# Tap-diagonal matmuls merged into larger runs, two transposes moved together and three filler matmuls added at the start of a convolution-plus-MLP kernel

## The chip, the cores and the metric

The kernel runs on one core of one Trainium2 chip. The metric is the device time of one execution in microseconds (us), as the median of several executions. A trace of one execution has its own clock, the *span*, from the first instruction to the last; it is about 1.8 us shorter than the device time (687.26 against 685.5 us in the profiled run of before). All positions below are us from the start of the span.

The engines are called by the profile's names: PE is the tensor engine, PEld its weight loads, ACT the scalar engine, DVE the vector engine, POOL GpSimd.

## The reference

```python
# x: (8, 4096, 192), weight: (8 heads, 7 taps)
w = exp(weight - max); w = w / (sum(w) + 1e-9)          # softmax over the 7 taps
out = einsum('hk,bskhg->bshg', w, windows_of(x))        # causal 7-tap convolution, a filter per head
# 32768 tokens of 192, d_ff = 2048
h = out @ w_in                                          # 192 -> 2048
g = h * sigmoid(beta * h)                               # beta per column of h
return g @ w_out                                        # 2048 -> 192
```

## The kernel before

The 32768 tokens are handled as two streams of 16384. Most of the time goes to 512-token steps: the DVE forms the seven-tap sum of x (tile `xc`), the PE multiplies by `w_in` into PSUM (`ph`), the ACT applies Silu (`g`), and the PE multiplies by `w_out` (`po`). The first steps are smaller: 128, 128 and 256 tokens, then four of 256. For the first three the PE does the convolution too, as matmuls with diagonal matrices of taps, because that is available sooner. That start is what the change touches.

```python
def warm(n, cols):                      # filler matmuls, result never read
    for _ in range(n):
        pin(nc.tensor.matmul(idle[:, 0, 0:cols], ones[:, 0:128], ones[:, 0:cols], start=True, stop=True))

warm(9, 256)
...
def conv_0(cv, b, k0=0, k1=K):          # two matmuls a tap, one for each stream
    for k in range(k0, k1):
        for s in range(NS):
            pin(nc.tensor.matmul(cv[s][:, 0:NK * 128], diag[half_of(s), k, :, :]...,
                xr[half_of(s), :, 128 * b + k:128 * b + k + 128], start=(k == 0), stop=(k == K - 1)))
...
t = transpose_0(pa[0], x0, 0)           # block 0: three transposes on the PE
take_0(t, 0, act=True)
warm(7, 128)
...
conv_0(b0, 0)                           # the first convolution, seven taps, nothing between them
...
def mm1_pair(i, u):                     # "large pair": two columns of w_in, one PSUM tile
    ph = psum_h.tile([128, NS, TILE], FP32, name="ph")       # psum_h has two buffers
    ...  6 matmuls, then 2 activations of 256 columns
...
for u in range(NF // 2):                # steps 0, 1 and 2
    mm1_pair(i, u)
    first_tile(i, u)                    # pieces of the convolution of blocks 1, 2, 3 (the change)
    ...  mm2 of earlier steps, as first_mm2 says
```

`first_tile(i, u)` is the list that the change rewrites. "Pair (0,5)" below means `mm1_pair(0, 5)`.

Of the kernel before, what the change touches and what calls it, by code (L numbers as in the profile page):

```python
# [19 lines left out]
def kernel(  # L20
# [9 lines left out]
    nc = tc.nc  # L30

    B, S, D = x.shape
    H, K = weight.shape
# [3 lines left out]
    NF = F // 128  # L37
    NK = 3
    Q = D // NK
    NS = 2  # L40
# [5 lines left out]
    def pin(ins):  # L46

        return tc.keep_in_program_order(ins)
# [27 lines left out]
    def load_x(j, s, b0=0, b1=NB, eng=None):  # L76
        if j not in xf_of:
            xf_of[j] = xf_pool.tile([128, NB, NS, D], FP32, name="xf")
        src = xs[s, TILE * j + 128 * b0:TILE * j + 128 * b1, :]
        pin((eng or nc.sync).dma_start(out=xf_of[j][:, b0:b1, s, :],  # L80
                                       in_=src.rearrange("(b p) d -> p b d", p=128)))

    def cast_x(j, s, b0=0, b1=NB, eng=None):
        if j not in xbf_of:
            xbf_of[j] = xbf_pool.tile([128, NB, NK, NS, Q], BF16, name="xb")
        pin((eng or nc.vector).tensor_copy(  # L86
            xbf_of[j][:, b0:b1, :, s, :].rearrange("p b k q -> p k b q"),
            xf_of[j][:, b0:b1, s, :].rearrange("p b (q k) -> p k b q", k=NK)))

    def new_xt(j):  # L90
        xt_of[j] = xt_pool.tile([128, NK, LEAD + TILE], BF16, name="xt")

    def transpose_x(j, b):
        if j not in xt_of:
            new_xt(j)
        c = LEAD + 128 * b
        pin(nc.sync.dma_start_transpose(
            out=xt_of[j][:, :, c:c + 128],
            in_=xbf_of[j][:, b, :, :, :].rearrange("p k s q -> p (k s q)")))
# [9 lines left out]
    def half_of(s):  # L109
        return slice(64 * s, 64 * s + 64)  # L110
# [9 lines left out]
    xb0 = consts.tile([128, 2, NS, D], BF16, name="xb0")  # L120
# [52 lines left out]
    def po_banks():  # L173
        return [po_bank(), po_bank()]
# [7 lines left out]
    def warm(n, cols):  # L182
        for _ in range(n):
            pin(nc.tensor.matmul(idle[:, 0, 0:cols], ones[:, 0:128], ones[:, 0:cols], start=True, stop=True))
# [3 lines left out]
    nmax = consts.tile([128, 1], FP32, name="nmax")  # L188
    tap_ps = cv0[:, 1, 0:K]
    pin(nc.tensor.matmul(tap_ps, sel.rearrange("h s g j -> h (s g j)"), taps, start=True, stop=True))  # L190
    pin(nc.vector.tensor_reduce(out=nmax, in_=tap_ps, axis=AX.X, op=ALU.max, negate=True))
    etap = consts.tile([128, K], FP32, name="etap")
    tsum = consts.tile([128, 1], FP32, name="tsum")
# [14 lines left out]
    def transpose_0(bank, src, b):  # L208

        bf = src.dtype == BF16  # L210
        t = (bank.bitcast(BF16) if bf else bank)[:, 0:NK * 128].rearrange("p (k t) -> p k t", k=NK)
        v = src[:, b, :, :].rearrange("p s d -> p (s d)").rearrange("p (m k) -> p k m", k=NK)
        for kk in range(NK):
            pin(nc.tensor.transpose(t[:, kk, :], v[:, kk, :], ident_b if bf else ident))
        return t

    def take_0(t, b, act=False):
        dst = xr[:, :, PAD + 128 * b:PAD + 128 * b + 128]
        if act:
            pin(nc.scalar.activation(dst, t, AF.Copy))  # L220
        else:
            pin(nc.vector.tensor_copy(dst, t))

    def conv_0(cv, b, k0=0, k1=K):

        for k in range(k0, k1):
            for s in range(NS):
                pin(nc.tensor.matmul(  # L228
                    cv[s][:, 0:NK * 128], diag[half_of(s), k, :, :].rearrange("p s q -> p (s q)"),
                    xr[half_of(s), :, 128 * b + k:128 * b + k + 128], start=(k == 0), stop=(k == K - 1)))  # L230

    def evac_0(cv, b, s, eng, k0=0, k1=NK):
        i, c = place[b]
        src = cv[s][:, 128 * k0:128 * k1].rearrange("p (k t) -> p k t", t=128)
        dst = xc_of[i][:, s, k0:k1, c:c + 128]
        if eng is nc.scalar:
            pin(nc.scalar.activation(dst, src, AF.Copy, scale=rsum))
        else:
            pin(eng.tensor_scalar_mul(dst, src, rsum))

    new_xt(0)
    pa = po_banks()
    pb = po_banks()
# [27 lines left out]
    def scale_w_out(c):  # L271
        pin(nc.vector.tensor_scalar_mul(w_out_s[:, c, :], w_out_f[:, c, :], rbeta[:, c:c + 1]))
# [219 lines left out]

    def first_tile(i, u):
        if (i, u) == (0, 1):
            conv_0(pb, 1, 0, 2)
        elif (i, u) == (0, 2):
            conv_0(pb, 1, 2, 4)
        elif (i, u) == (0, 3):
            take_0(transpose_0(pa[0], xb0, 0), 2)
            conv_0(pb, 1, 4, 5)  # L500
        elif (i, u) == (0, 4):
            take_0(transpose_0(pa[1], xb0, 1), 3)
            conv_0(pb, 1, 5, K)
            for s in range(NS):
                evac_0(pb, 1, s, nc.vector)
            for c in range(4):
                scale_w_out(c)
        elif (i, u) == (0, 5):
            conv_0(pa, 2, 0, 2)
        elif (i, u) == (0, 6):  # L510
            conv_0(pa, 2, 2, 5)
        elif (i, u) == (0, 7):
            conv_0(pa, 2, 5, K)
            for s in range(NS):
                evac_0(pa, 2, s, nc.vector)
            for c in range(4, 8):
                scale_w_out(c)
        elif (i, u) == (1, 0):
            conv_0(pb, 3, 0, 2)
        elif (i, u) == (1, 1):  # L520
            conv_0(pb, 3, 2, 5)
        elif (i, u) == (1, 2):
            conv_0(pb, 3, 5, K)
            for s in range(NS):
                evac_0(pb, 3, s, nc.vector)
            for c in range(8, NF):
                scale_w_out(c)
        elif (i, u) == (1, 6):
            new_xt(1)
            ts_ = [transpose_0(pb[b], xb1, b) for b in range(2)]  # L530
            for b in range(2):
                pin(nc.vector.tensor_copy(xt_of[1][:, :, LEAD + 128 * b:LEAD + 128 * b + 128], ts_[b]))
            pin(nc.vector.tensor_copy(xt_of[0][:, :, TILE + LEAD - PAD:],
                                      xr[:, :, TILE:].bitcast(FP32)))
        elif (i, u) == (1, 7):
            for s in range(NS):
                cast_x(1, s, 2, NB)
            for b in range(2, NB):
                transpose_x(1, b)
            for j in (2, 3):  # L540
                for s in range(NS):
                    load_x(j, s)
# [2 lines left out]

    prs_0 = ((0, 0), (1, 0))
    first_mm2 = {}
    for key, us, cuts in (((0, 0), [(1, u) for u in range(3, 8)], (0, 4, 8, 12, 13, 16)),
                          ((1, 0), [(2, 1), (2, 2)], (0, 8, 16)),
                          ((0, 1), [(2, 3), (2, 4)], (0, 8, 16)),  # L550
                          ((1, 1), [(2, 5), (2, 6), (2, 7)], (0, 5, 10, 16))):
        for (i, u), c0, c1 in zip(us, cuts, cuts[1:]):
            first_mm2[(i, u) + key] = range(c0, c1)

    for i in range(n_steps):
        plan = mm2_plan(i - 1) if NP <= i <= NQ else [[] for _ in range(NF)]
        new_g(i, 0)
        if i < NP:
            new_g(i, 1)
        if i < NP:  # L560
            for u in range(NF // 2):
                mm1_pair(i, u)
                first_tile(i, u)
                for ph in (0, 1):
                    for j in range(i):
                        for fc in first_mm2.get((i, u, j, ph), ()):
                            mm2(j, prs_0, ph, fc)
                if i == 2:
                    vector_work(i, 1300, flush=u == NF // 2 - 1)
            continue  # L570
        for u in range(NF):
            if u == NF // 2:
                new_g(i, 1)
            mm1(i, u)
            for t in plan[u]:
                mm2(i - 1, *t)
                if t[1] == 1 and t[2] == NF - 1:
                    budget -= 2 * (D + 60) / 0.96
            if i > NQ:
                mm2_quarters(NM)  # L580
            vector_work(i, 1307 * steps[i][1] // TILE, flush=u == NF - 1)
# [30 lines left out]
```

## Time and profile before

| what | value |
|---|---|
| device time, three runs | 687.62 to 687.64 us, median 687.63 |
| span of the profiled run | 685.5 us |
| first activation of step 0 | 8.63 us |
| tap sum of the second 512-token step complete | 90.59 us (88.52 + 2.07 below) |
| first activation of that step | 91.16 us |
| from there to the end | 594.3 us |

The busy time of each engine in four stretches of the kernel before (columns: stretch, its length, then busy us and instruction count of PE, PEld, DVE, ACT and POOL, then the granted tensor clock, DMA share and GB/s):

```profile
8.63:12.63 4.00, 3.87 (x48) 2.47 (x44) 1.40 (x6) 3.86 (x10) 3.57 (x5) 1.00 1.14 254
12.63:21.57 8.94, 8.94 (x138) 7.04 (x135) 8.32 (x27) 8.35 (x22) 3.19 (x5) 1.00 1.05 256
21.57:90.64 69.07, 68.47 (x1270) 59.41 (x1266) 68.29 (x118) 68.23 (x97) 0.00 (x0) 1.00 0.47 128
90.64:670.00 579.36, 579.36 (x10728) 410.65 (x10731) 466.31 (x730) 497.81 (x448) 0.00 (x0) 1.00 0.36 90
```

In the third stretch PE, DVE and ACT all look full. A share cannot tell which of them sets the pace; the waits can. In the fourth the PE alone is full. The timeline of the ACT before (start, duration, what, count, and in brackets the idle time before it with its releaser):

```profile
8.63 4.00 ACT L323 ACTIVATE gp<-ph,beta 128x256 bf16<-128x256 f32 x10 [0.54 <-PE ph L319]
12.97 8.81 ACT L323 ACTIVATE gp<-ph,beta 128x256 bf16<-128x256 f32 x22 [0.35 <-PE ph L319]
74.16 16.36 ACT L340 ACTIVATE g<-ph,beta 128x1024 bf16<-128x1024 f32 x16 [0.35 <-PE ph L336]
91.16 2.34 ACT L340 ACTIVATE g<-ph,beta 128x1024 bf16<-128x1024 f32 x2 [0.64 <-PE ph L336]
```

At 91.16 the ACT waited for the PE, and the PE timeline of before shows why: it waited for the DVE's tap sum.

```profile
89.63 0.76 PE L336 MATMUL ph<-xc,w_in_s 64*64 64x512 bf16 x8
90.64 0.41 PE L336 MATMUL ph<-xc,w_in_s 64*64 64x512 bf16 x4 [0.25 <-DVE xc L302]
```

The DVE timeline of before, from its last start-up work (the eviction of block 3 at 17.20 us, that is, its copy out of PSUM) to that tap sum:

```profile
17.20 1.14 DVE L239 TENSOR_SCALAR xcp<-po,rsum 128x384 bf16<-128x384 f32 x2 [0.25 <-PE po L228]
18.25 1.96 DVE L272 TENSOR_SCALAR w_out_s<-w_out_f,rbeta 128x192 bf16<-128x192 f32 x8
20.25 0.62 DVE L532 COPY xt<-po 128x384 bf16<-128x384 bf16 x2
21.57 0.50 DVE L86 CAST xb<-xf 128x384 bf16<-128x384 f32 x1 [0.21 <-DMA xf<-in_x_dram]
22.18 0.75 DVE L300 TENSOR_SCALAR acc<-xt,tapn 128x768 f32<-128x768 bf16 x1
...
88.52 2.07 DVE L302 SCALAR_TENSOR_TENSOR xc<-xt,tapn,acc 128x512 bf16<-128x512 bf16 x3
```

Last, two lines of the PE timeline in the first convolution of before. Successive taps start 0.32 us apart; later in the trace a tap takes 0.18 us. The tensor clock is at half rate here.

```profile
5.38 0.52 PE L228 MATMUL po<-xr,diag 64*128 64x384 f32 x1
5.70 0.52 PE L228 MATMUL po<-xr,diag 64*128 64x384 f32 x1
```

### The profile page before, as it was taken

How to read it: one execution, taken by the hardware profiler on the slowest of the kernel's cores; microseconds unless marked ns; L12 is line 12 of the kernel's file. 1: busy time of each engine (PE TensorE's matmuls, PEld its weight loads, DVE VectorE, ACT ScalarE, POOL GpSimd, SP SyncE). 2: the span in 40 equal slices, each digit the busy share in tenths (PEclk: the TensorE clock that was granted, in tenths of full speed). 3: DMA queues.
4: the chain of work that ended last, by engine and by line, in shares of the span. 5: the costliest groups of instructions: out<-in, count | busy, mean ns of one | idle time of the engine just before them, and what ended most of it. 6: DMA issues, size and time to landing. Idle time of an engine off the chain costs nothing.

```text
span 685.5 us, 26898 instructions
## 1 busy us (share of the span) xinstructions
PE 681.0 (99%) x12365; PEld 497.0 (73%) x12365; DVE 552.8 (81%) x906; ACT 583.9 (85%) x585; POOL 14.5 (2%) x26
## 2 busy tenths in 40 slices
PE   9999999999999999999999999999999999999998
PEld 7799767777777777777777777777777777777777
DVE  5999999999988889878889888889888888875102
ACT  7999988888888888888888888888888888888881
POOL 8000000000000000000000000000000000000000
PEclk9999999999999999999999999999999999999999
DMA  9664334354423344423344323444323443220213
GB/s 201 176 164 121 96 93 104 86 118 117 114 75 71 100 112 117 104 64 87 102 116 118 93 68 91 103 117 118 81 65 102 106 117 72 59 54 9 49 48 93
DMA packets 149872, 66.82 MB, mean 97 GB/s; under 512 B 112592, under 2 KB 149152, under 8 KB 149760
## 3 DMA queue, kind: packets, MB, share of 16 engines
q1 hardware_dynamic: 146448, 61.08, 35.5%
q0 software_dynamic: 3168, 3.93, 2.8%
q8 instruction: 96, 1.57, 1.0%
q14 instruction: 16, 0.13, 0.1%
q10 hardware_dynamic: 144, 0.10, 0.1%
HBM read 28.32 MB, written 25.17 MB: 78 GB/s over the span
## 4 chain that ended last, share of the span: by engine, by line
PE 86%; DVE 9%; DMA 2%; issue 1%; POOL 1%; POOLq 0%; DVEq 0%
PE po L414 42%; PE ph L336 42%; DVE acc L302 5%; PE po L452 2%; DMA xf<-in_x_dram 1%; DMA w_in_s<-in_moe_w_in_dram 1%; DVE o_sp L374 1%; DVE xb L86 1%; DVE acc L300 1%; DVE xc L302 1%; POOL w_in_s L113 0%; DVE w_out_q L275 0%; POOL xb L131 0%; POOL sel L146 0%; DVE xt L291 0%
## 5 line engine op out<-in xcount | busy, mean ns | idle before, releaser
L340 ACT ACTIVATE g<-ph,beta 128x1024 bf16<-128x1024 f32 (+1 forms) x528 | 557.4, 1062 | 82.3 <-PE ph L336 65.2
L336 PE MATMUL ph<-xc,w_in_s 64*64 64x512 bf16 (+2 forms) x5856 | 624.6, 369 | 0.6 <-ACT g L323 0.3
L414 PE MATMUL po<-g,w_out_q 64*64 64x512 bf16 x5376 | 578.9, 376 | 0.0
L336 PEld LDWEIGHTS <-w_in_s 64*64 64x64 bf16 (+1 forms) x5856 | 320.8, 104 | 105.5 <-issue 1.4
L414 PEld LDWEIGHTS <-w_out_q 64*64 64x64 bf16 x5376 | 312.4, 105 | 67.5
L302 DVE SCALAR_TENSOR_TENSOR acc<-xt,tapn,acc 128x512 f32<-128x512 bf16 (+1 forms) x455 | 311.1, 752 | 0.6
L431 DVE STREAM_TRANSPOSE o_sb<-po 128x512 f32<-128x512 f32 x84 | 74.4, 886 | 113.0 <-PE po L414 112.9
L302 DVE SCALAR_TENSOR_TENSOR xc<-xt,tapn,acc 128x512 bf16<-128x512 bf16 (+1 forms) x91 | 64.0, 754 | 0.1
L86 DVE CAST xb<-xf 128x768 bf16<-128x768 f32 (+1 forms) x62 | 48.3, 816 | 0.2 <-DMA xf<-in_x_dram 0.2
L300 DVE TENSOR_SCALAR acc<-xt,tapn 128x512 f32<-128x512 bf16 (+1 forms) x91 | 40.5, 480 | 1.1
L368 PE MATMUL po<-w_out_s,g 64*128 64x192 bf16 x640 | 41.2, 243 | 0.0
L368 PEld LDWEIGHTS <-g 64*128 64x128 bf16 x640 | 31.3, 94 | 3.5
L374 DVE COPY o_sp<-po 128x192 f32<-128x192 f32 x32 | 10.2, 350 | 7.3 <-PE po L452 7.3
L319 PE MATMUL ph<-xcp,w_in_s 64*128 64x256 bf16 (+1 forms) x144 | 14.7, 306 | 0.2
L323 ACT ACTIVATE gp<-ph,beta 128x256 bf16<-128x256 f32 x32 | 12.4, 479 | 1.3 <-PE ph L319 0.9
L452 PEld LDWEIGHTS <-g 128*128 128x128 bf16 x128 | 10.5, 98 | 0.4 <-issue 0.4
L452 PE MATMUL po<-w_out_s,g 128*128 128x192 bf16 x128 | 10.7, 246 | 0.0
L323 ACT ACTIVATE g<-ph,beta 128x512 bf16<-128x512 f32 x16 | 9.6, 691 | 0.1
L319 PEld LDWEIGHTS <-w_in_s 64*128 64x128 bf16 x144 | 6.7, 94 | 3.3 <-issue 0.9
L228 PE MATMUL po<-xr,diag 64*128 64x384 f32 x49 | 8.8, 398 | 0.0
L368 PE MATMUL po<-w_out_s,gp 64*128 64x192 bf16 x128 | 7.7, 243 | 0.0
L368 PEld LDWEIGHTS <-gp 64*128 64x128 bf16 x128 | 6.0, 94 | 1.8
(53 smaller groups left out, 61.5 us busy)
## 6 DMA issues: line engine op xcount, KB each, us to landing
xf<-in_x_dram SPq DMA_DIRECT2D x60, 384.0 KB, 4.6
out_dram<-o_sb SPq DMA_DIRECT2D x112, 192.0 KB, 4.3
out_dram<-o_sp SPq DMA_DIRECT2D x12, 192.0 KB, 4.3
xt<-xb SPq DMA_TRANSPOSE x122, 2.4
w_out_f<-in_moe_w_out_dram POOLq DMA_DIRECT2D x4, 384.0 KB, 7.0
w_in_s<-w_in_s POOLq DMA_DIRECT2D x4, 192.0 KB, 7.1
out_dram<-o_sp SPq DMA_DIRECT2D x8, 96.0 KB, 1.6
w_in_s<-in_moe_w_in_dram POOLq DMA_DIRECT2D x4, 144.0 KB, 5.2
```

Of the source, the lines that this page charges most:

```text
L86: pin((eng or nc.vector).tensor_copy(xbf_of[j][:, b0:b1, :, s, :].rearrange("p b k q -> p k b q"), xf_of[j][:, b0:b1, s, :].rearrange("p b ...
L300: pin(nc.vector.tensor_scalar_mul(a, src, w))
L302: pin(nc.vector.scalar_tensor_tensor(out=xc_of[i][:, k0:k1, 0:n] if k == K - 1 else a, in0=src, scalar=w, in1=a, op0=ALU.mult, op1=ALU.add))
L319: pin(nc.tensor.matmul(ph[:, h, 0:NS * n], w_in_s[half_of(h), kk, ts(fcs[h], 128)], xc_of[i][half_of(h), :, kk, :], start=(kk == 0), stop= ...
L323: pin(nc.scalar.activation(g_at(i, fcs[h])[:, :, 0:n], ph[:, h, 0:NS * n].rearrange("p (s t) -> p s t", s=NS), AF.Silu, scale=beta[:, fcs[ ...
L336: pin(nc.tensor.matmul(ph[m0:m1, s, 0:n], w_in_s[half_of(s), kk, 128 * fc + m0:128 * fc + m1], xc_of[i][half_of(s), kk, 0:n], start=(kk == ...
L340: pin(nc.scalar.activation(g_at(i, fc)[:, :, 0:n], ph[:, :, 0:n], AF.Silu, scale=beta[:, fc:fc + 1]))
L368: pin(nc.tensor.matmul(po[q][:, 0:D], g_at(i, fc)[r, s, ts(b, 128)], w_out_s[r, fc, :], start=(phase == 0 and fc == 0), stop=(phase == 1 a ...
L374: pin(nc.vector.tensor_copy(dst, po[:, 0:D]))
L414: pin(nc.tensor.matmul(po_of[i, m][half_of(s), 0:n], w_out_q[half_of(r), fc, m, :], g_at(i, fc)[half_of(r), s, 0:n], start=(first and fc = ...
L431: pin(nc.vector.transpose(osb_of[i][:, 0:n // L, :, m], po_of[i, m][:, 0:n].rearrange("p (b l) -> p b l", l=L)))
L452: pin(nc.tensor.matmul(po[:, 0:D], g_at(i, fc)[:, s, ts(b, 128)], w_out_s[:, fc, :], start=(fc == 0), stop=(fc == NF - 1)))
```

## The change

The intent: fewer changes between the small diagonal matmuls and the large pairs (ten runs become six), block 1 finished before the PE turns to the late transposes, and three fillers so that the PE has no thin spot before the first transposes. The last part, a new distribution of the first `mm2` over the pairs of step 1, follows from block 3's being finished two pairs earlier.

```diff
--- before.py
+++ after.py
@@ -188,6 +188,7 @@
     nmax = consts.tile([128, 1], FP32, name="nmax")
     tap_ps = cv0[:, 1, 0:K]
     pin(nc.tensor.matmul(tap_ps, sel.rearrange("h s g j -> h (s g j)"), taps, start=True, stop=True))
+    warm(3, 128)
     pin(nc.vector.tensor_reduce(out=nmax, in_=tap_ps, axis=AX.X, op=ALU.max, negate=True))
     etap = consts.tile([128, K], FP32, name="etap")
     tsum = consts.tile([128, 1], FP32, name="tsum")
@@ -492,38 +493,30 @@
 
     def first_tile(i, u):
         if (i, u) == (0, 1):
-            conv_0(pb, 1, 0, 2)
+            conv_0(pb, 1, 0, 4)
         elif (i, u) == (0, 2):
-            conv_0(pb, 1, 2, 4)
+            conv_0(pb, 1, 4, K)
         elif (i, u) == (0, 3):
-            take_0(transpose_0(pa[0], xb0, 0), 2)
-            conv_0(pb, 1, 4, 5)
-        elif (i, u) == (0, 4):
-            take_0(transpose_0(pa[1], xb0, 1), 3)
-            conv_0(pb, 1, 5, K)
+            t23 = [transpose_0(pa[b], xb0, b) for b in range(2)]
+            for b in range(2):
+                take_0(t23[b], 2 + b)
             for s in range(NS):
                 evac_0(pb, 1, s, nc.vector)
+        elif (i, u) == (0, 5):
+            conv_0(pa, 2, 0, 4)
+        elif (i, u) == (0, 6):
+            conv_0(pa, 2, 4, K)
+            for s in range(NS):
+                evac_0(pa, 2, s, nc.vector)
             for c in range(4):
                 scale_w_out(c)
-        elif (i, u) == (0, 5):
-            conv_0(pa, 2, 0, 2)
-        elif (i, u) == (0, 6):
-            conv_0(pa, 2, 2, 5)
         elif (i, u) == (0, 7):
-            conv_0(pa, 2, 5, K)
-            for s in range(NS):
-                evac_0(pa, 2, s, nc.vector)
-            for c in range(4, 8):
-                scale_w_out(c)
+            conv_0(pb, 3, 0, 4)
         elif (i, u) == (1, 0):
-            conv_0(pb, 3, 0, 2)
-        elif (i, u) == (1, 1):
-            conv_0(pb, 3, 2, 5)
-        elif (i, u) == (1, 2):
-            conv_0(pb, 3, 5, K)
+            conv_0(pb, 3, 4, K)
             for s in range(NS):
                 evac_0(pb, 3, s, nc.vector)
-            for c in range(8, NF):
+            for c in range(4, NF):
                 scale_w_out(c)
         elif (i, u) == (1, 6):
             new_xt(1)
@@ -545,7 +538,7 @@
 
     prs_0 = ((0, 0), (1, 0))
     first_mm2 = {}
-    for key, us, cuts in (((0, 0), [(1, u) for u in range(3, 8)], (0, 4, 8, 12, 13, 16)),
+    for key, us, cuts in (((0, 0), [(1, u) for u in range(2, 8)], (0, 3, 6, 9, 12, 13, 16)),
                           ((1, 0), [(2, 1), (2, 2)], (0, 8, 16)),
                           ((0, 1), [(2, 3), (2, 4)], (0, 8, 16)),
                           ((1, 1), [(2, 5), (2, 6), (2, 7)], (0, 5, 10, 16))):
```

## The prediction

> **What bounds the kernel.** I read three stretches off the timeline and the table of busy time by stretch.
> - 8.63 to about 90 us: the ScalarE activations run nearly back to back (0.40 us each in the first two steps, 0.65 us in the 256-row steps). Their only recorded waits for TensorE are 0.54 us at 8.63, 0.35 at 12.97, 0.35 at 74.16 and 0.64 at 91.16.
> - 21.57 to 90.6 us: VectorE is busy 68.29 of 69.07 us. It starts when a DMA delivers `xf`: issued at 12.68, landed 8.86 us later, and VectorE had waited 0.21 us for it. It ends with `xc` at 90.6 us, for which TensorE waits 0.25 us. The chain of waits runs through exactly these pieces.
> - 90.64 to 670 us: TensorE is busy all the time (579.36 of 579.36 us).
>
> **What the change does.** It touches only the first 21 us. No work is removed; three matmuls of 128 columns are added.
> - *Fewer switches on TensorE.* Diagonal runs of 2 taps (4 matmuls) take 0.44 us to the next pair's start and runs of 3 taps (6) take 0.62, so a pair of matmuls costs 0.09 x 2 and each run carries about 0.08 us of its own (estimate from these two). Ten runs become six: about 0.3 us less. The two late transposes each begin 0.43 us after their pair where a diagonal run begins 0.25 after: one such 0.18 us goes. Together about 0.5 us of TensorE time between 8 and 17 us.
> - *Block 1 finished before the transposes*, block 3 two pairs earlier. ScalarE's 0.35 us wait at 12.97 should go. The seven-tap halves (8 matmuls, about 0.80 us) plus a pair (0.25) exceed ScalarE's 0.80 us per pair, but two buffers absorb it; perhaps 0.1 to 0.2 us returns as a wait near pair (1,0).
> - *Fillers.* At 2.8 to 3.3 us TensorE has little work. The diagonal pairs at 4.90 to 6.98 come every 0.32 us, later ones every 0.18: half clock, then full. The Trainium skill, "TensorE: Matmul & The Clock Gate", Part 1, says a busy window of about 3.4 us is needed to leave half rate and that the window runs freely; this trace agrees with the two rates, but not necessarily with a moved switch. If the fillers fill the deciding window, up to 1.1 us goes from the first convolution; otherwise they cost up to 0.3 us. I lean slightly to no effect.
> - *VectorE.* Its twelve remaining output-weight scalings (0.245 us each) now stand in one run after block 3's eviction. I estimate that eviction at about 16.1 us and VectorE ready for `xf` at about 21.1, still before 21.55.
>
> **How much is critical.** TensorE and ScalarE get ahead by 0.3 to 1 us by 17 us, but step 90.6 us waits for VectorE's sum of taps, whose start is set by a DMA that no TensorE instruction releases and whose 69 us are saturated. So the gain turns into a longer wait of TensorE for `xc` near 90 us. The total hardly moves.
>
> **Prediction.** 687.5 us, 80% range 687.0 to 687.8. Faster by over 2%: 0.005; within 2%: 0.99; slower by over 2%: 0.005.
>
> **What would show each step.** The first activation of step 0 at 8.63 us or earlier; the 0.35 us wait at 12.97 gone; VectorE's second `xf` cast still starting at 21.5 to 21.6 after a DMA wait; the tap sum ending at 90.5 to 90.7; TensorE's wait for `xc` there grown from 0.25 us; the stretch after it unchanged at about 595 us.
>
> **What would make it wrong.** `xf` landing at another time; block 3's eviction after 16.5 us, so that VectorE reaches `xf` late (slower by that much); a VectorE chain with hidden waits for TensorE (faster, at most about 1 us); the clock falling back to half rate.

## The result

The change is neutral. In the same rounds the changed kernel took 687.76 us (687.23 to 688.16, 4 runs) and the kernel before 687.62 (687.52 to 687.64, 4 runs). The ratio is 1.0002, with a 95% interval from 0.9984 to 1.0019. (A ratio here is the mean time of one kernel's fast runs over the mean of the other's fast runs of the same rounds, so it is not quite the ratio of the two medians.) What stands out is the spread: 0.9 us for the changed kernel. It is not the change's own: in the three later sets of rounds the nine runs of the kernel before spread over 0.8 to 1.4 us.

The lines of the changed kernel that answer to those above; its source lines are numbered one higher from the fillers on. First the ACT timeline:

```profile
8.81 4.82 ACT L324 ACTIVATE gp<-ph,beta 128x256 bf16<-128x256 f32 x12 [0.54 <-PE ph L320]
13.96 1.72 ACT L324 ACTIVATE gp<-ph,beta 128x256 bf16<-128x256 f32 x4 [0.33 <-PE ph L320]
15.91 6.30 ACT L324 ACTIVATE gp<-ph,beta 128x256 bf16<-128x256 f32 x16 [0.23 <-PE ph L320]
74.49 16.36 ACT L341 ACTIVATE g<-ph,beta 128x1024 bf16<-128x1024 f32 x16 [0.35 <-PE ph L337]
91.27 2.34 ACT L341 ACTIVATE g<-ph,beta 128x1024 bf16<-128x1024 f32 x2 [0.42 <-PE ph L337]
```

The start is 0.18 us later. The wait at 12.97 is gone, but two others came, 0.33 us before pair (0,6) and 0.23 before pair (1,0). At 74 us the ACT is 0.33 us behind before; at 91 us only 0.11, because the wait there fell from 0.64 to 0.42 us. The DVE and PE timelines of the changed kernel:

```profile
16.31 1.14 DVE L240 TENSOR_SCALAR xcp<-po,rsum 128x384 bf16<-128x384 f32 x2
20.69 0.62 DVE L525 COPY xt<-po 128x384 bf16<-128x384 bf16 x2 [0.49 <-PE po L215]
21.30 0.89 DVE L86 CAST xb<-xf 128x384 bf16<-128x384 f32 x2
22.31 0.75 DVE L301 TENSOR_SCALAR acc<-xt,tapn 128x768 f32<-128x768 bf16 x1
...
88.64 2.07 DVE L303 SCALAR_TENSOR_TENSOR xc<-xt,tapn,acc 128x512 bf16<-128x512 bf16 x3
```

```profile
3.31 0.50 PE L184 MATMUL ph<-const-bfloat16-1.0 128*128 128x128 bf16 x3
3.61 0.85 PE L215 MATMUL po<-ident,x 128*128 128x128 f32 x3
5.62 0.52 PE L229 MATMUL po<-xr,diag 64*128 64x384 f32 x1
5.94 0.52 PE L229 MATMUL po<-xr,diag 64*128 64x384 f32 x1
...
90.76 0.41 PE L337 MATMUL ph<-xc,w_in_s 64*64 64x512 bf16 x4 [0.17 <-DVE xc L303]
```

Three things are visible. Block 3's eviction (the 16.31 line) did come earlier than before (17.20 us). The DVE's chain of tap sums nevertheless began 0.13 us later (22.31 against 22.18). And the fillers delayed the first transposes by 0.30 us, from 3.31 to 3.61, while the taps still come 0.32 us apart, so they did not bring the full clock earlier in this execution. The stretch from the first activation near 91 us to the end is 594.3 us in both traces.

### The profile page after: what moved, and what is told of

It reads as the page before. It is cut to its first block, busy times and chain, and to the rows that moved or that the text cites. A ratio compares the mean times of both kernels' runs of the same rounds, so it can differ in the third digit from the quotient of the medians.

```text
span 685.6 us, 26903 instructions
## 1 busy us (share of the span) xinstructions
PE 681.1 (99%) x12368; PEld 498.1 (73%) x12368; DVE 552.4 (81%) x906; ACT 583.8 (85%) x585; POOL 14.5 (2%) x26
## 4 chain that ended last, share of the span: by engine, by line
PE 89%; DVE 9%; issue 1%; ACT 0%; DVEq 0%
PE po L415 42%; PE ph L337 42%; DVE acc L303 5%; PE po L453 2%; DVE xb L86 1%; DVE o_sp L375 1%; PE ph L320 1%; DVE acc L301 1%; DVE xc L303 1%; PE po L229 1%; PE ph L184 0%; DVE w_out_q L276 0%; PE ph L229 0%; ACT gp L324 0%; PE po L215 0%
```

## The experiments

Three theories were to be told apart. *Floor*: what the PE and the ACT gain or lose before 90 us is hidden by the DVE's chain of tap sums. *Pass-through*: the start-up shift reaches the end in full. *Clock phase*: the moment at which the tensor clock rises differs from execution to execution and is worth more than the change.

### The fillers alone, and the regrouping alone

Edits:

```diff
  # e1: the kernel before
  pin(nc.tensor.matmul(tap_ps, ..., taps, start=True, stop=True))
+ warm(3, 128)
```

```diff
  # e2: the changed kernel
- warm(3, 128)
```

> The kernel before plus only the three fillers. Floor theory (the vector engine's chain of taps, which starts with the xf cast at 21.6 us and ends at 90.6, hides what the tensor and scalar engines gain or lose earlier): the first activation of step 0 comes at 8.81 us as in the changed kernel (8.63 before), the clock rises at about 7.0 to 7.1 us as in both, and the time stays within 0.15 us of the kernel before. Rival (the start-up shift passes through to the end): 0.2 us slower.

> The changed kernel without the fillers. If the regrouping alone starves the scalar engine (two seven-tap halves against two buffers), the activations of pair (1,4) begin about 0.25 us later than before (18.31 us before, 18.95 in the changed kernel, of which 0.18 is the fillers': so about 18.7), and scalar waits of 0.2 to 0.3 us near pairs (0,6) and (1,0) remain. Floor theory: time within 0.15 us of before. Rival: if the regrouping saves what the prediction said (0.5 us of tensor time) and the fillers alone lose it, pair (1,4) begins before 18.3 us and the time is up to 0.3 us lower.

Measured, with before at 687.36 us (686.87 to 687.69, 9 runs): fillers alone 687.0 (its four fast runs 686.76 to 687.01), ratio 0.9993 (0.998 to 1.0007); regrouping alone 687.76 (687.07 to 688.08), ratio 1.0004 (0.9991 to 1.0017). Both contain 1. The profiled execution of e1, of 3681.92 us, explains nothing (see the last section). The regrouping alone shows the clock phase at once. Its ACT timeline:

```profile
9.37 4.82 ACT L323 ACTIVATE gp<-ph,beta 128x256 bf16<-128x256 f32 x12 [1.08 <-PE ph L319]
14.52 1.71 ACT L323 ACTIVATE gp<-ph,beta 128x256 bf16<-128x256 f32 x4 [0.34 <-PE ph L319]
16.46 6.31 ACT L323 ACTIVATE gp<-ph,beta 128x256 bf16<-128x256 f32 x16 [0.23 <-PE ph L319]
91.86 2.34 ACT L340 ACTIVATE g<-ph,beta 128x1024 bf16<-128x1024 f32 x2 [0.45 <-PE ph L336]
```

It has no fillers, so it should have started as early as before. But the trace's record of the granted clock has the rise to full rate at 9.38 us, against 6.97 us in the trace of before, and so the first activation came 0.74 us later. The two waits of the changed kernel (0.34 and 0.23 us) are here without fillers: they belong to the regrouping.

### Moving copies off the DVE, to GpSimd

```diff
- pin(nc.vector.tensor_copy(w_out_q[...], w_out_s[...]))     # 12 copies, at 74 us
+ pin(nc.gpsimd.tensor_copy(w_out_q[...], w_out_s[...]))     # after pair (1,7)
```

> The kernel before with the twelve copies that split w_out by thirds moved from the vector engine to the idle GpSimd, early (about 20 us). Floor theory: the vector chain loses 2.6 us of work, the tap sum of the first 512-row steps ends 2 us or more ahead of its use, the scalar engine's wait of 0.64 us at 91.16 shrinks to about 0.2, and the kernel is 0.3 to 0.5 us faster than before. Rival (the vector chain is not what sets the time at 90 us): same time as before within 0.1 us. If GpSimd's copies slow the vector engine, its tap operations at 21 to 40 us get longer than 1.03 us.

> The changed kernel with the same twelve copies on GpSimd. Floor theory: with the vector floor gone the later start shows in full, so this one is 0.3 to 0.45 us slower than e3_before_pool (the scalar front of the changed kernel is 0.33 us behind at 74 us), while the two without the move differ by about 0.1. Rival: the difference stays at 0.1 us or less.

Measured: e3 688.1 us (687.9 to 689.74), ratio 1.0015 (1.0002 to 1.0029); e4 687.97 (686.5 to 688.11), ratio 1.0005 (0.9993 to 1.0018). The gain expected of e3 did not come, for a reason that has nothing to do with the theories. The copies ran while the DVE scaled `w_out`. In e3's trace, DVE and POOL:

```profile
18.20 4.30 DVE L272 TENSOR_SCALAR w_out_s<-w_out_f,rbeta 128x192 bf16<-128x192 f32 x8
18.70 2.12 POOL L275 COPY w_out_q<-w_out_s 128x256 bf16<-128x256 bf16 x6
```

The same eight scalings took 1.96 us before; the PE waited 1.5 us for them and the ACT 2.0 us. So this pair doesn't test the floor. What e4's trace gives instead is the other end of the clock phase. In its first convolution the taps are 0.18 us apart from the second on:

```profile
5.29 0.34 PE L229 MATMUL po<-xr,diag 64*128 64x384 f32 x1
5.47 0.34 PE L229 MATMUL po<-xr,diag 64*128 64x384 f32 x1
```

Its first activation came at 7.82 us and its span was 684.7 us, the shortest of the traces with correct results. The source of this kernel up to there is the changed kernel's, whose own trace had 8.81.

### A gate, to hold the clock phase still

```diff
+ late = consts.tile([128, 256], FP32, name="late")
+ for _ in range(28):
+     pin(nc.vector.memset(late, 0.0))       # holds back sel, which the taps need
  sel = consts.tile(...)
- warm(9, 256)
+ warm(44, 256)
```

> The kernel before, held back at its start: 28 small memsets on the vector engine (about 7.5 us) delay the selector that the taps and everything after need, while 44 instead of 9 filler matmuls keep the tensor engine busy, so its clock must be full before the first transposes. If the run-to-run spread of up to 1 us comes from the moment at which the tensor clock rises (seen at about 4.3 to 5, 6.84, 6.97, 7.10 and 9.38 us in five traces), the five times of this kernel agree within 0.15 us, and the seven diagonal pairs of the first convolution come every 0.18 us. Rival (the spread comes from the input transfers): the spread stays at 0.5 us or more. About 6 to 7.5 us slower than the kernel before, which is the price of the gate and of no interest.

> The same gate on the changed kernel without its three fillers. If the vector chain hides the regrouping, its time equals g1_gate_before within 0.1 us although its scalar front at pair (1,4) is about 0.25 us later, counted from the first activation. Rival: the scalar front passes through, 0.25 us slower than g1. Rival of the prediction: 0.2 to 0.3 us faster.

> The same gate on the whole changed kernel. With the clock already full the three fillers can only cost: 3 x 0.055 = 0.17 us ahead of the first transposes, so 0.1 to 0.2 us slower than g2_gate_regroup. If they still make it faster, they do something other than hold the clock up.

> g1_gate_before with six casts of x (0.8 us each on the vector engine, between 29 and 57 us of the kernel before) moved to the idle GpSimd. Floor theory: 4.8 us leave the vector chain, the scalar engine's wait of 0.64 us at the step boundary near 91 us (plus the gate) shrinks to about 0.2, and the kernel is 0.3 to 0.6 us faster than g1. Rival (the vector chain sets nothing): equal within 0.1 us. GpSimd may slow the vector engine where both run, by 0.1 to 0.2 us a cast.

Measured: g1 697.85 us (697.52 to 698.27), g2 699.14 (697.94 to 700.2), g3 698.15 (697.51 to 698.75), g4 698.91 (697.94 to 701.4), beside before at 686.88 (686.32 to 687.68). The gate failed. It opened about 4 us later than I had worked out; the PE timeline of g1:

```profile
0.78 7.52 PE L187 MATMUL ph<-const-bfloat16-1.0 128*128 128x256 bf16 x44 [0.78 <-PEq L599]
12.41 0.38 PE L193 MATMUL ph<-taps,sel 8*128 8x7 f32 x2 [4.11 <-POOL sel L149]
```

In those 4.11 idle us the clock fell back. The clock record of g1 reads: full from 5.92 us for 6.827 us, half for 3.413 us, full again from 16.16. So the spread did not collapse, and the differences between g1, g2 and g3 can't be read as the cost of the parts. In g4, GpSimd again slowed the DVE: five tap operations of 128x768 took 7.51 us beside the casts, against 5.24 in g1. Why the two slow each other was not tested.

The failed gate is still of use, as a look at the clock. The stretches of full and half clock are multiples of 3.41 us. In g2's trace the clock rose at 3.64 us, with fillers running from 0.78; in before and after, with thinner work in the same window, it did not rise until about 7.

### A shorter DVE chain without moving anything (wrong result)

```diff
- for k in range(K) for p in parts]
+ for k in range(K) if k != 3 or i > NQ + 1 for p in parts]    # one tap less in six steps
```

> The kernel before with one of the seven taps left out in the first six steps that the vector engine convolves (wrong result on purpose): about 8 us leave the vector chain between 22 and 90 us and nothing is added to any engine. Counted from the first activation to the end of the span, which a trace gives free of the clock's phase, the kernel before takes 676.85 us. Floor theory: the scalar engine's wait at the boundary near 91 us shrinks from 0.64 to about 0.2 us, and this stretch is 676.3 to 676.5 us. Rival (the vector chain sets nothing): 676.8 to 676.9.

> The same omission in the changed kernel (wrong result on purpose), which takes 676.77 us from its first activation to the end. Floor theory: the stretch falls too, and the regrouping's own cost to the scalar front (0.15 us at 74 us, counted from the first activation) is no longer hidden: 0.1 to 0.2 us longer than the same stretch of f1_before_six_taps. Rival: equal or shorter than f1's, if the regrouping costs nothing.

This takes work from the DVE in the stretch from 22 to 90 us and adds none anywhere. The results are wrong (relative error 0.13 in both). The times (687.02 and 686.85 us against 686.89 for before, ratios 0.9998 with 0.9985 to 1.0012, and 0.9995 with 0.9981 to 1.0009) can't show a few tenths under the clock phase. The traces can, if counted from the first activation. The ACT timeline of f1, then of f2:

```profile
74.06 18.78 ACT L340 ACTIVATE g<-ph,beta 128x1024 bf16<-128x1024 f32 x18 [0.35 <-PE ph L336]
93.02 1.11 ACT L340 ACTIVATE g<-ph,beta 128x1024 bf16<-128x1024 f32 x1 [0.18 <-PE ph L336]
```

```profile
74.27 18.78 ACT L341 ACTIVATE g<-ph,beta 128x1024 bf16<-128x1024 f32 x18 [0.35 <-PE ph L337]
93.23 1.11 ACT L341 ACTIVATE g<-ph,beta 128x1024 bf16<-128x1024 f32 x1 [0.18 <-PE ph L337]
```

Before, the group stopped after 16 activations and waited 0.64 us (0.42 in the changed kernel). With the DVE early it runs on through 18 without a stop. From the first activation to the end, f1 takes 676.14 us against 676.85 for before, and f2 676.49 against 676.77 for the changed kernel. So the tap sum does set the time at 91 us in both kernels. Without that limit the regrouping costs 0.35 us (676.49 - 676.14), twice what I expected of f2. (With the limit it costs nearly as much, as the table of all traces will show.) The ACT is already that far behind when the 512-token steps begin: 65.75 us after its first activation in f2, 65.39 in f1. f1's 0.71 us is also more than expected: 0.57 of it lies at 91 us and 0.14 before 74 us (65.39 against 65.53). The likely reason for the 0.14 is that in f1's trace `xf` landed in time. With no DMA wait its tap sums began 13.21 us after the first activation, against 13.55 in before. The DVE timeline of f1:

```profile
20.25 0.62 DVE L532 COPY xt<-po 128x384 bf16<-128x384 bf16 x2
20.87 0.89 DVE L86 CAST xb<-xf 128x384 bf16<-128x384 f32 x2
21.87 0.75 DVE L300 TENSOR_SCALAR acc<-xt,tapn 128x768 f32<-128x768 bf16 x1
```

### Fillers alone and the whole change once more

No new edit: e6 is e1, e7 is the changed kernel.

> The kernel before plus the three fillers, again, since its profile fell into an odd slow run. If the fillers make early windows count as busy, the clock rises earlier in more executions: median 0.2 to 0.5 us below the kernel before of the same rounds, as the four fast runs of the first time were (687.0 against 687.36). Rival (chance): within 0.15 us of the kernel before. A profile with the rise at about 7 us has the first activation at 8.8, with a rise at 4 to 5 us at 7.8.

> The changed kernel again, beside the others on one chip. By the parts so far (fillers about minus 0.3 to minus 0.4, regrouping about plus 0.3) it is within 0.3 us of the kernel before, with a spread of 0.7 us or more. If the fillers' gain holds here too, its median lies below the kernel before; its profile gives another pair of rise and first activation, and 676.8 us from the first activation to the end.

Measured: e6 687.54 us (686.19 to 687.74), ratio 1.0001 (0.9989 to 1.0014); e7 687.25 (686.74 to 687.97), ratio 1.0003 (0.9989 to 1.0017); before 686.89 (686.66 to 687.64). The advantage of e1 did not come again, so by the times no effect of the fillers is established either way. e6's trace caught an early rise (4.45 us), and its first activation came at 7.85 us, as in e4. Yet its span was 685.2 us, only 0.3 below before. At pair (0,5) the PE waited 0.4 us for a piece of `w_in`, and the ACT, with a wait of 0.99 us, lost its whole lead there (step 2 begins at 21.90 us against 21.84). Block 3's eviction came no earlier either (17.30 us). The 0.3 us that remain are those that before lost to `xf`: here the tap sums began at 21.94 us, without a DMA wait.

```profile
13.09 8.76 ACT L324 ACTIVATE gp<-ph,beta 128x256 bf16<-128x256 f32 x22 [0.99 <-PE ph L320]
```

### All traces together

From the timelines and the clock records, in us; "pair (1,7)" is its first activation on the ACT, "tap sums begin" the start of the DVE's chain (its first `acc`), "tap sum" the end of the DVE's `xc` for the second 512-token step, "activation after it" the first that reads its product. E4, e3 and g4, in which GpSimd disturbed the DVE, and the other gated runs are left out.

| run | fillers | clock rises | first activation | pair (1,7) | tap sums begin | tap sum | activation after it | end of span |
|---|---|---|---|---|---|---|---|---|
| before | no | 6.97 | 8.63 | 20.94 | 22.18 | 90.59 | 91.16 | 685.48 |
| changed | yes | 7.10 | 8.81 | 21.38 | 22.31 | 90.71 | 91.27 | 685.58 |
| e2, regrouping alone | no | 9.38 | 9.37 | 21.93 | 22.86 | 91.30 | 91.86 | 686.18 |
| e6, fillers alone | yes | 4.45 | 7.85 | 21.01 | 21.94 | 90.35 | 90.91 | 685.22 |
| e7, changed again | yes | 6.33 | 8.47 | 21.07 | 22.00 | 90.38 | 90.96 | 685.28 |
| f1, before, six taps | no | 7.06 | 8.67 | 20.94 | 21.87 | 85.71 | 90.49 | 684.80 |
| f2, changed, six taps | yes | 6.45 | 8.52 | 21.15 | 22.08 | 85.91 | 90.70 | 685.01 |

In the first five rows the activation follows the tap sum by 0.56 to 0.58 us, whatever the ACT was doing: the tap sum decides. In the last two it follows by 4.8 us: there the ACT's own queue decides. In every row 594.3 us remain from that activation to the end. The rows f1 and changed have almost the same rise (7.06 and 7.10) and show what the fillers cost when they don't move the clock: 8.81 - 8.67 = 0.14 us.

The tap sum decides, but it does not hide the start-up, because the DVE's chain is no clock of its own. It takes 68.4 us in each of the first five rows, and it begins 0.93 us after the ACT's first activation of pair (1,7) in every row but that of before (and 0.93 or 0.94 us after it in the four gated traces). In before it is 1.24 us: the second `xf` cast waited for its DMA until 21.57 us, where f1 has it at 21.28. In the four regrouped traces the DVE waits 0.38 to 0.50 us for the PE's late transposes just before the chain; in before and e6 the eviction of block 3, from which the DVE runs on, waits 0.25 and 0.34 us for the PE.

So *pass-through* fits these traces and *floor* does not. Pair (1,7) comes 12.56 to 12.63 us after the first activation with the regrouping and 12.27 to 12.31 without (13.16 in e6, with its wait for `w_in`). The 0.3 us between them reach the end of the span: from pair (1,7) to there it is 664.20 to 664.25 us in changed, e2, e6 and e7, and 664.54 in before. That before and changed end within 0.1 us of each other is due to the 0.31 us that before's trace lost to `xf`. How often an execution of before loses them is not known, and the times can't show 0.3 us.

## Why the prediction was right, and where it wasn't

- **The total** (687.5 us, range 687.0 to 687.8; measured 687.76) was right, its mechanism only in part. The tap sum near 90 us does decide, as the six-tap runs show. That it swallows what happens at the start is not so: the chain begins a fixed 0.93 us after pair (1,7), except where `xf` is late. The total held because the shifts are small (0.3 us from the regrouping, 0.14 from the fillers), against a spread of 0.8 us and more; that the two profiled spans agree within 0.1 us is luck.
- **"TensorE and ScalarE get ahead by 0.3 to 1 us by 17 us" was wrong, in sign.** They fell behind: 0.18 us at the first activation and 0.43 us by the end of step 1 (22.27 against 21.84 us). The tensor engine did finish the convolution earlier, with block 3's eviction at 16.31 us against 17.20, so the saved switches are real. What was mis-sized is the term "two buffers absorb it; perhaps 0.1 to 0.2 us returns": the seven-tap halves starved the ACT for 0.33 + 0.23 us. In the changed trace the pairs that carry eight diagonal matmuls take 1.15, 1.17 and 1.05 us from pair start to pair start, while the ACT needs 0.73 us a pair when it is fed (16.79 to 17.52 us). Two buffers don't bridge that. In the 1.17 us of pair (0,5) lies a wait of 0.30 us for a piece of `w_in`, but the regrouping alone has the same ACT wait there (0.34 us) without that transfer's wait.
- **"The 0.35 us wait at 12.97 gone"**: right, but replaced by those two. In e6 the same pair waits for a piece of `w_in`, so it stands close to a transfer as well, which the prediction missed.
- **Fillers**: the chance was named (a moved clock, or a cost of up to 0.3 us). In the traced run they cost: 0.30 us at the transposes and 0.18 at the first activation (0.14 beside f1). What the prediction missed is that the moment of the rise is not a property of the kernel. Up to there all kernels without fillers have the same source, and so have all with them; yet the rise varied between 6.84 (e3) and 9.38 us without, and between 4.45 and 7.10 with them.
- **"The second `xf` cast at 21.5 to 21.6 after a DMA wait"**: wrong. In the changed kernel the DVE waited 0.49 us for the PE's transposes instead, and the casts ran at 21.30 without a DMA wait. That the chain then began within 0.13 us of before is luck: before lost 0.31 us to a late `xf` (1.24 against 0.93 us after pair (1,7)).
- **"The start is set by a DMA that no TensorE instruction releases"** is the step that failed. It holds for the trace of before only, and there for the last 0.31 us. In all other rows of the table the chain follows work that the PE releases. In the traces of the changed kernel it starts 13.50 and 13.53 us after the first activation, against 13.21 in f1, so both the clock phase and the cost of the regrouping pass through to the end.
- **"TensorE's wait for `xc` grown from 0.25 us"**: it shrank to 0.17, which follows from the wrong sign above. **Tap sum at 90.5 to 90.7**: 90.71. **The stretch after it unchanged, about 595 us**: 594.3 in both.

Open remains whether the fillers make early rises more frequent. Rises at about 4.5 us or before were seen only with fillers (e6, and e4, which has no clock record, but whose seven fillers at 4.25 us took 0.58 us against 0.95 at 4.01 us in before), the one at 9.38 us only without, but nine ungated traces are too few, and the times of e1 and e6 disagree. Nor was it tested what makes the times spread: the rise of the clock differs between the traces, but so do late transfers (`xf` in before, `w_in` in e6), and the gate that should have held the clock still failed. No version beat both kernels beyond the spread.

## What to carry to other kernels

Before moving work on an engine that looks full, find the wait that ends last at the end of that stretch; here a single line (`0.25 <-DVE xc`) names the DVE. Then ask what releases the start of that engine's work: a chain of fixed length hides nothing if it begins when the work before it ends, and one trace in which a DMA came last does not show that it always does. When small matmuls are put between large ones that feed a second engine through two buffers, look at the longest gap between two feeds and not only at the sum: here bundling saved PE time and cost the ACT more. For effects below the run-to-run spread, compare traces from a fixed event (here the first activation) and not the times.

## What the Trainium skill lacked or had wrong

- "TensorE: Matmul & The Clock Gate", Part 1, gives a free-running window of 3.41 us. The runs agree: full and half clock lasted 6.827 and 3.413 us in g1. The page does not say how busy a window must be to count. In g2 a window with fillers from 0.78 us to its end at 3.64 lifted the clock; in before, one ending near 3.55 us (the rise at 6.97 less 3.41) with fillers until 2.86 and then the taps and a few transposes did not.
- The same part calls the run-to-run variation of the switch ±500 ns and tells the reader not to fit to a cold count. Its figure is for matmuls issued back to back, which this start is not. Here the rise lay between 6.84 and 9.38 us in four traces with the same source up to there (before, f1, e3, e2), and the first activation between 8.58 and 9.37 us, while the spans of before and changed differ by 0.1 us.
- The same part, "Seeing it yourself", reports the clock stuck low for over 50 us. One execution of e1 may be such a case, from end to end: 3681.92 us instead of 687. It has no clock record at all, but neither has e4, which ran fast, so a low clock is not shown; only the PE's own work was slow. The mean of the large matmuls was 1379 ns against 369 in before, while the DVE's tap operations kept their length (756 ns against 752). Its line among the groups:

```profile
L337 PE MATMUL ph<-xc,w_in_s 64*64 64x512 bf16 (+2 forms) x5856 | 3360.8, 1379 | 0.0
```

- The same caveat does not say that the record may lack the start: the first event in the trace of before is the rise at 6.97 us, and the profile's granted clock is 1.00 from 0 us on, while the taps at 5 to 7 us ran 0.32 us apart against 0.18. The spacing of the matmuls showed it.
